# The first expert item's later rows: transposed by VectorE during the last query steps

## The chip, the core and the metric

The kernel runs on one core of a Trainium2 chip. Its time is the device time of one execution in microseconds; 267.24 us is the median of three runs, which lie between 267.22 and 270.07.

## The reference, cut to what matters

The inputs are q, k and v of shape 4 x 8 x 576 x 64 (batch, head, row, column), a random matrix omega of 128 x 64, and a mixture of eight experts with w1 of 512 x 1024 and w2 of 1024 x 512 each. All is float32.

```python
def phi(x):                                   # x = q or k, times 64 ** -0.25
    h = einsum('bhsd,md->bhsm', x, omega) - sum(x * x, -1) / 2
    return exp(h - max(h, -1)) / sqrt(128)
kv, z = einsum('bhsm,bhsd->bhmd', phi(k), v), sum(phi(k), 2)
attn = einsum('bhsm,bhmd->bhsd', phi(q), kv) / (einsum('bhsm,bhm->bhs', phi(q), z) + 1e-06)
x = attn.transpose(0, 2, 1, 3).reshape(2304, 512)
logits = x @ w_gate                           # 8 experts; each row goes to the largest
h = maximum(x_of_expert @ w1[e], 0)           # at most capacity = 576 rows for each expert
out[row] = gate[row] * (h @ w2[e])
```

## The kernel before, in words

**Attention.** The kernel first works through the keys in 18 steps, then through the 18 query tiles of 128 rows, in a software pipeline: step t projects tile t (`pjq`), transposes tile t - 2 on the matrix engine PE (`qtr`), turns it into phi(q) by exponentials on ScalarE (`qpT`, L798) and sums tile t - 3 against kv (`qacc`, L634). `normalise` (L645 to L660) then divides on VectorE, giving the tile `xr`, adds up the routing logits `lg` and stores the tile's rows in the DRAM tensor `x_d`. Steps 18 to 20 have no projection; the last two have fewer of the other parts. PSUM is scarce: `qtr` uses banks 3 and 4, `qacc` a single pair of banks, and the first layer of the experts goes round banks 0, 1 and 2.

**Experts.** Each batch of 576 rows is one item: the rows of a batch go to one expert. Four items run one after another. For an item the first layer (`mm1`, L668) has 16 groups: eight blocks `f` of 128 hidden columns times two halves of the rows, 256 and 320 of them. Every float32 product is made of three products of a high and a low part: `xhi` and `xlo` are the rows with features on partitions, `w1hi` and `w1lo` the weights. The high part comes from a copy on ScalarE with rounding, the low part from a subtraction on VectorE. After a group ScalarE writes the relu's high part (`hhii`, L680) and VectorE its low part (`hloi`, L683). The second layer (`mm2`, L842 to L844) gives `y`.

**The first item.** Its expert is read from the logits of row 0 as soon as tile 0 is done, so its weights load and are split (on GpSimd) during the query steps. Its rows 0 to 255 are taken from the tiles `xr` of query steps 3 and 4 while these are in SBUF: at steps 5 to 8 (`FIRST_AT`) PE transposes blocks of 64 rows beside the query transposes (`xtri`, L742), and `copy_x` makes the two parts. Rows 256 to 575 come back from `x_d`: at step 15 `first_rows` (L625) issues one load of 768 KB into `xg`, and ahead of the groups k = 0, 1 and 2 of the item's loop `transpose_x` has PE transpose 128, 128 and 64 of them (`xtri`, L398). Three groups, blocks 0 to 2 of the first half, are issued earlier, one in each of steps 18 to 20 (`AHEAD`); the loop begins with blocks 3 to 5 of the first half, and then comes block 0 of the second.

**Later items.** Their rows come by `load_x` (L380): four transfers, each for 32 partitions, which put rows in blocks of 32 with 512 bytes of a row in each partition (`xz`, a view of `xg`). `turn_x` (L386) transposes 32 x 32 blocks on VectorE into `xt`, ScalarE copies `xt` to `xhi` and VectorE subtracts to `xlo`. With it feature 4p + k lies on partition p in chunk k, so `load_w` loads these items' w1 by rows 4p + k, while the first item's features are 128k + p and its w1 is loaded in that order.

**Order.** The schedule is written by hand: each engine works off its instructions in the order of the program, and waits where an operand isn't ready. SyncE (SP) issues nearly all transfers, in the order of the program: at step 15 a store of `x_d`, then the rows; in the steps after it a store and a quarter of w2 each. Routing work of VectorE is spread over the first item's groups (`listing`).

Of the kernel before, what the change touches and what calls it, by code (L numbers as in the profile page):

```python
# [9 lines left out]
F32 = mybir.dt.float32  # L10
# [4 lines left out]
ALU = mybir.AluOpType  # L15
# [4 lines left out]
B, H, S, D, M = 4, 8, 576, 64, 128  # L20
# [4 lines left out]
SLOTS = 576  # L25
FIRST_CUTS = [0, 128, 384, 768, 1152]
SUB = 128
NSUB = 5
REST = SLOTS - 4 * SUB
NB, NBA = SLOTS // 32, 8  # L30
# [26 lines left out]
def attention_moe(ctx, tc, kT, qT, va, om, wg, w1, w2, cap, ident, tri, desc, lst, tab0, out):  # L57
    nc = tc.nc
# [8 lines left out]
    x_d = dram.tile([N + REST, DM], F32, name="x_d")  # L67
# [9 lines left out]
    SM = 5  # L77
# [272 lines left out]

    def load_w(i, c, ev, chunks_of="(k p)"):
        if i == 1:
            src = w1[ds(ev, 1), :, c * 256 : (c + 1) * 256].rearrange(f"o {chunks_of} f -> p (o k) f", p=128)
        else:
            src = w2[ds(ev, 1), c * 256 : (c + 1) * 256, :].rearrange("o (k p) f -> p (o k) f", p=128)
        nc.sync.dma_start(w_raw[i][c], src)
# [18 lines left out]
                in_offset=bass.IndirectOffsetOnAxis(ap=big["idx"][0:n, i, 2:3], axis=0),  # L377
            )

    def load_x(row):  # L380
        src = x_d[ds(row, SLOTS), :].rearrange("(b r) (q c) -> q r b c", r=32, q=4)
        for q in range(4):
            nc.sync.dma_start(big["xz"][32 * q : 32 * q + 32, :, :], src[q])


    def turn_x(b0, b1):  # L386
        t = big["xt"][:, 0 : b1 - b0, :].rearrange("p b (k r) -> p b k r", k=4)
        nc.vector.transpose(t, big["xz"][:, b0:b1, :].rearrange("p b (a k) -> p b k a", k=4))
        t = t.rearrange("p b k r -> p k b r")
        hi, lo = (big[x][:, :, 32 * b0 : 32 * b1].rearrange("p k (b r) -> p k b r", r=32) for x in ("xhi", "xlo"))  # L390
        nc.scalar.copy(hi, t)
        nc.vector.tensor_tensor(lo, t, hi.bitcast(F32), op=ALU.subtract)

    def transpose_x(i, nm, at):
        n = sub_n[i]
        tr = pair(f"xtr{nm}{i}") if at is None else bank(at, f"xtr{nm}{i}")
        for k in range(4):
            nc.tensor.transpose(  # L398
                tr[:, k * n : (k + 1) * n], big["xg"][0:n, i, k * 128 : (k + 1) * 128], id_sb[0:n, 0:n]
            )  # L400
        yield from copy_x(tr, i * SUB, n)
# [221 lines left out]
    xr_l = {}  # L623

    def first_rows():  # L625
        nc.sync.dma_start(
            big["xg"][:, 2:, :], x_d[2 * SUB : NSUB * SUB, :].rearrange("(i p) d -> p i d", p=SUB)
        )

    def numer(t, qpT, acc):  # L630
        for p in range(NP):
# [11 lines left out]

    def normalise(t, acc):
        xr = small.tile([128, ROW, H], F32, tag="xr", name=f"xr{t}", bufs=4)  # L645
        if t < 2:
            xr_l[t] = xr
        av = acc.rearrange("p (i x) -> p i x", i=2)[:, :, 0 : NP * ROW].rearrange("p i (h c) -> p c i h", c=ROW)
        den = small.tile([128, H], F32, tag="den", name=f"den{t}")
        nc.vector.tensor_scalar(den.rearrange("p (i h) -> p i h", i=2), av[:, D, :, :], EPS, None, op0=ALU.add)  # L650
        rec = small.tile([128, H], F32, tag="rec", name=f"rec{t}")
        nc.vector.reciprocal(rec, den)
        nc.vector.tensor_tensor(
            xr.rearrange("p c (i h) -> p c i h", i=2),
            av,
            rec.rearrange("p (i h) -> p i h", i=2).unsqueeze(1).to_broadcast([128, ROW, 2, NP]),
            op=ALU.mult,
        )
        nc.vector.tensor_reduce(lg[:, t, :], xr[:, D + 1 : ROW, :], op=ALU.add, axis=AX.X)
        nc.sync.dma_start(x_d[t * 128 : (t + 1) * 128, :], xr[:, 0:D, :].rearrange("p c h -> p (c h)"))  # L660

    HALVES = [(0, 256), (256, SLOTS)]

# [23 lines left out]
    def h_tiles(nm):  # L687
        return [
            hpool.tile([128, 8, w], dt, tag=t, name=f"{t}{nm}")
            for t, w, dt in (("hhi", 4 * SUB, F32R), ("hlo", 4 * SUB, F32R), ("hf", REST, F32))  # L690
        ]
# [8 lines left out]
    for n in range(NK + NT + 3):  # L700
# [20 lines left out]
        if 0 <= t - 2 < NT:  # L721
            d = d_l.pop(t - 2)
            trs = [bank(3 + i, f"qtr{n}{i}") for i in range(2)]

            parts = [
                [(trs[i][:, u * 64 : (u + 1) * 64], d[64 * i : 64 * i + 64, u, :], i) for u in range(H)] for i in range(2)
            ]

            if t in FIRST_AT:
                k0 = FIRST_AT.index(t)  # L730
                i = k0 % 2
                tr = bank(SM, f"xtri0{k0}")
                rows = slice(64 * i, 64 * i + 64)
                x0 = xr_l[k0 // 2][:, 0:D, :].rearrange("p c h -> p (c h)")
                parts[i][0:0] = [
                    (tr[:, k * 64 : (k + 1) * 64], x0[rows, k * 128 : (k + 1) * 128], i) for k in range(4)
                ]
                start(copy_x(tr, 64 * k0, 64))
            for x in chain(*zip_longest(*parts)):
                if x is not None:  # L740
                    rows = slice(64 * x[2], 64 * x[2] + 64)
                    nc.tensor.transpose(x[0], x[1], id_sb[rows, rows])  # L742
        if t == NT:
            h0 = h_tiles("i0")
        if t >= NT:
            mm1(*AHEAD[t - NT], *h0, "i0")
        run()

# [143 lines left out]
    with ExitStack() as ifs:  # L892
        for j in range(B):
            nm = f"i{j}"
            last = j == B - 1
            if j > 0:
                ifs.enter_context(tc.If(nd > j - 1))
            hhi, hlo, hf = h_tiles(nm) if j > 0 else h0
            if j > 0:
                row_a = nc.scalar.value_load(resd[0:1, 1, j - 1 : j], min_val=0, max_val=N - S)  # L900
            out_j = [out[0:SLOTS, :]] * 2 if j == 0 else [out[ds(r, SLOTS), :] for r in (row, row_a)]
            sc = sc_b[:, 0, :] if j == 0 else sc_j[:, j - 1, :]

            def put(i, n, y, out_j=out_j):

                k = int(i == NSUB - 2)
                (nc.sync, nc.scalar)[k].dma_start(out_j[k][i * SUB : i * SUB + n, :], y[0:n, :])

            def prefetch():
                nonlocal row  # L910
                if last:
                    return
                ev = nc.sync.value_load(resd[0:1, 0, j : j + 1], min_val=0, max_val=E - 1)
                row = nc.sync.value_load(resd[0:1, 1, j : j + 1], min_val=0, max_val=N - S)
                load_x(row)
                for c in range(4):
                    load_w(1, c, ev, "(p k)")
                yield
                for c in range(4):
                    load_w(2, c, ev)  # L920
                yield

            pre = prefetch()
            for k, (f, half) in enumerate(STEPS[j > 0]):

                if j == 0 and k < 3:
                    for _ in transpose_x(2 + k, nm, (SM, 3, None)[k]):
                        pass
                mm1(f, half, hhi, hlo, hf, nm)
                if j == 0:  # L930

                    listing(5 if k > 2 else 1)
                if j > 0 and k == 0:
                    next(pre, 0)
                if j == 0 and k < 6:
                    zero_out(k)
                if half == 0:
                    continue
                for i, c in HI_AT[j > 0].get(f, ()):
                    split_w_hi(i, c)  # L940
                for i, c in LO_AT[j > 0].get(f, ()):
                    split_w_lo(i, c)
            if j == 0:
                for _ in il:
                    pass
                next(pre, 0)
            for n, i in enumerate((NSUB - 1, *range(NSUB - 1))):
                pt = mm2(i, hhi, hlo, nm) if n > 0 else mm2_rest(hf, nm)
                if n == 0:
                    next(pre, 0)  # L950
                finish(i, pt, nm, sc[:, i : i + 1], put)

                if not last:
                    if n == 1:
                        turn_x(0, NBA)
                    for c in ((), (0,), (1,), (2, 3), ())[n]:
                        split_w_hi(1, c)
                        split_w_lo(1, c)
                    if n == 2:
                        turn_x(NBA, NB)  # L960
            if j == 0:
                nd = nc.values_load(resd[0:1, 2, 0:1], min_val=0, max_val=B - 1)
                nl = nc.values_load(resd[0:1, 2, 1:2], min_val=0, max_val=N)
# [68 lines left out]
    with ExitStack() as ifs:  # L1032
# [3 lines left out]
        for j in range(J):  # L1036
            nm = f"l{j}"
# [2 lines left out]
            sv = nc.sync.value_load(res[0:1, 1, j : j + 1], min_val=0, max_val=(E - 1) * REG + N)  # L1040
            load_idx(sv)
            for c in range(4):
                load_w(1, c, ev)
            for c in range(4):
                load_w(2, c, ev)
            gather()
# [71 lines left out]
```

## Time and profile before

| | |
|---|---|
| median of three runs | 267.24 us |
| profiled execution | 267.57 us |
| its span, first to last instruction | 265.7 us |
| PE busy | 257.0 us, 97% of the span |
| VectorE (DVE) busy | 166.2 us, 63% |
| ScalarE (ACT) busy | 150.5 us, 57% |
| GpSimd (POOL) busy | 36.6 us, 14% |

The profile is of one execution. Times in its rows are microseconds from the start of the span. PE is the matrix engine, SPq the transfer queue of SyncE. An arrow in a row goes from what is read to what is written, and L with a number is a line of the kernel. The chain of waits is followed back from the last instruction to what released each one, so a piece on it could not have begun sooner.

### The profile page before, as it was taken

How to read it: one execution, taken by the hardware profiler on the slowest of the kernel's cores; microseconds unless marked ns; L12 is line 12 of the kernel's file. 1: busy time of each engine (PE TensorE's matmuls, PEld its weight loads, DVE VectorE, ACT ScalarE, POOL GpSimd, SP SyncE). 2: the span in 40 equal slices, each digit the busy share in tenths (PEclk: the TensorE clock that was granted, in tenths of full speed). 3: DMA queues.
4: the chain of work that ended last, by engine and by line, in shares of the span. 5: the costliest groups of instructions: out<-in, count | busy, mean ns of one | idle time of the engine just before them, and what ended most of it. 6: DMA issues, size and time to landing. Idle time of an engine off the chain costs nothing.

```text
span 265.7 us, 7584 instructions
## 1 busy us (share of the span) xinstructions
PE 257.0 (97%) x3070; PEld 228.9 (86%) x3070; DVE 166.2 (63%) x329; ACT 150.5 (57%) x377; POOL 36.6 (14%) x54
## 2 busy tenths in 40 slices
PE   7999999999999999999999999999999999999990
PEld 6989999999999998999868889996888999958870
DVE  3889888869998984745762854443337443533570
ACT  4678878899999984436412465442254445224251
POOL 2100000243369892000000000000000000000000
PEclk9999999999999999999999999999999999999997
DMA  6999770045876677791079939900831892037211
GB/s 181 377 375 360 270 255 2 5 122 182 282 237 215 246 254 256 255 384 63 2 146 295 379 142 207 319 4 3 265 122 56 157 312 76 0 84 253 79 48 51
DMA packets 34130, 48.66 MB, mean 183 GB/s; under 512 B 2274, under 2 KB 21986, under 8 KB 34082
## 3 DMA queue, kind: packets, MB, share of 16 engines
q1 hardware_dynamic: 33506, 47.18, 56.2%
q10 hardware_dynamic: 576, 0.85, 0.9%
q8 instruction: 28, 0.46, 0.7%
q14 instruction: 20, 0.16, 0.2%
HBM read 36.10 MB, written 11.93 MB: 181 GB/s over the span
## 4 chain that ended last, share of the span: by engine, by line
PE 90%; ACT 3%; DVE 3%; issue 1%; ACTq 0%; DVEq 0%
PE hi L675 9%; PE hi L676 9%; PE hi L677 9%; PE yi L842 8%; PE pjk L165 8%; PE yi L843 8%; PE yi L844 8%; PE qacc L634 7%; PE pjq L165 6%; PE kacc L236 4%; PE kp L236 4%; PE qtr L742 3%; PE yi2r L854 1%; PE yi0r L854 1%; PE yi1r L854 1%
## 5 line engine op out<-in xcount | busy, mean ns | idle before, releaser
L675 PE MATMUL hi<-xhi,w1hi 128*128 128x256 f32 (+1 forms) x192 | 57.2, 298 | 0.3 <-DVE hloi L683 0.3
L676 PE MATMUL hi<-xhi,w1lo 128*128 128x256 f32 (+1 forms) x192 | 56.4, 294 | 0.0
L677 PE MATMUL hi<-xlo,w1hi 128*128 128x256 f32 (+1 forms) x192 | 56.3, 293 | 0.0
L683 DVE SCALAR_TENSOR_TENSOR hloi<-hi,hhii 128x256 fp32r<-128x256 f32 x48 | 20.2, 422 | 40.4 <-ACT hfi L682 24.5
L680 ACT ACTIVATE hhii<-hi 128x256 fp32r<-128x256 f32 x48 | 18.4, 385 | 42.8 <-PE hi L677 42.8
L842 PE MATMUL yi<-w2hi,hhii 128*128 128x512 f32 x96 | 37.7, 393 | 0.0
L843 PE MATMUL yi<-w2hi,hloi 128*128 128x512 f32 x96 | 37.4, 389 | 0.0
L844 PE MATMUL yi<-w2lo,hhii 128*128 128x512 f32 x96 | 37.4, 389 | 0.0
L675 PEld LDWEIGHTS hi<-xhi,w1hi 128*128 128x128 f32 x192 | 36.0, 188 | 0.8 <-DVE hloi L683 0.5
L676 PEld LDWEIGHTS hi<-xhi,w1lo 128*128 128x128 f32 x192 | 36.0, 188 | 0.1
L677 PEld LDWEIGHTS hi<-xlo,w1hi 128*128 128x128 f32 x192 | 36.0, 187 | 0.0
L182 DVE TENSOR_REDUCE mx<-pjk 128x4 f32<-128x512 f32 (+1 forms) x38 | 23.3, 654 | 5.5 <-PE pjk L165 5.5
L792 POOL TENSOR_TENSOR d<-d,mx 128x512 f32<-128x512 f32 x18 | 18.7, 1039 | 53.7 <-DVE mx L182 49.4
L165 PE MATMUL pjk<-om_s,kraw 64*128 64x128 f32 x288 | 24.9, 308 | 0.5 <-DVE ex L779 0.5
L773 ACT ACTIVATE ex<-pjk,mx 128x128 f32<-128x128 f32 x72 | 20.6, 368 | 7.4 <-DVE mx L182 7.2
L842 PEld LDWEIGHTS yi<-w2hi,hhii 128*128 128x128 f32 x96 | 18.0, 188 | 6.1 <-issue 2.4
L165 PEld LDWEIGHTS pjk<-om_s,kraw 64*128 64x128 f32 x288 | 21.3, 210 | 1.7 <-PE pjk L165 0.8
L634 PE MATMUL qacc<-kv_sb,qpT 128*64 128x73 f32 x576 | 22.5, 229 | 0.2 <-DVE e L587 0.2
L165 PE MATMUL pjq<-om_s,qraw 64*128 64x128 f32 x288 | 21.4, 284 | 0.1
L844 PEld LDWEIGHTS yi<-w2lo,hhii 128*128 128x128 f32 x96 | 18.0, 188 | 3.8
L634 PEld LDWEIGHTS qacc<-kv_sb,qpT 128*64 128x64 f32 x576 | 19.8, 136 | 1.6 <-PE qtr L742 0.3
L843 PEld LDWEIGHTS yi<-w2hi,hloi 128*128 128x128 f32 x96 | 18.0, 188 | 3.7
(141 smaller groups left out, 405.4 us busy)
## 6 DMA issues: line engine op xcount, KB each, us to landing
w1raw<-w SPq DMA_DIRECT2D x16, 512.0 KB, 8.3
w2raw<-w SPq DMA_DIRECT2D x16, 512.0 KB, 6.4
qraw<-qT SPq DMA_DIRECT2D x6, 768.0 KB, 6.3
x_d<-xr SPq DMA_DIRECT2D x18, 256.0 KB, 2.9
v<-va SPq DMA_DIRECT2D x7, 650.0 KB, 6.9
kraw<-kT SPq DMA_DIRECT2D x6, 576.0 KB, 6.6
xg<-x_d SPq DMA_DIRECT2D x12, 288.0 KB, 5.5
out<-zero_sb SPq DMA_DIRECT2D x4, 768.0 KB, 5.7
```

The costliest lines, as they stand in the source:

```text
L165: nc.tensor.matmul(banks[i][:, k * M : (k + 1) * M], parts[k][rows, :], om_s[rows, :], start=True, stop=True)
L182: nc.vector.tensor_reduce(mx[:, a : a + src.shape[1]], src, op=ALU.max, axis=AX.X, negate=True)
L236: nc.tensor.matmul(acc[f : f + 64, i * 2 * VW + o : i * 2 * VW + o + (z - a) * VW], ex[:, 4 * i + k, f : f + 64], v[:, i, a * VW : z * VW] ...
L634: nc.tensor.matmul(acc[r : r + 64, i * 512 + p * ROW : i * 512 + (p + 1) * ROW], qpT[:, r // 64, (4 * i + p) * 64 : (4 * i + p) * 64 + 64] ...
L675: nc.tensor.matmul(pt, whi_[:, k, fs], xhi[:, k, sl], start=(k == 0), stop=False)
L676: nc.tensor.matmul(pt, wlo_[:, k, fs], xhi[:, k, sl], start=False, stop=False)
L677: nc.tensor.matmul(pt, whi_[:, k, fs], xlo[:, k, sl], start=False, stop=(k == 3))
L683: nc.vector.scalar_tensor_tensor(hlo[:, f, sl], pt[:, 0:w], 0.0, hhi[:, f, sl].bitcast(F32), op0=ALU.max, op1=ALU.subtract)
L773: nc.scalar.activation(ex[:, o + k, :], q[0][:, k * M : (k + 1) * M], AF.Exp, bias=mx[:, o + k : o + k + 1], scale=1.0)
L842: nc.tensor.matmul(pt, hhi[:, f, sl], w2hi, start=(f == 0), stop=False)
L843: nc.tensor.matmul(pt, hlo[:, f, sl], w2hi, start=False, stop=False)
L844: nc.tensor.matmul(pt, hhi[:, f, sl], w2lo, start=False, stop=(f == 7))
```

## The change

The first item's rows 256 to 575 are loaded as the later items' rows are, by four transfers into blocks 8 to 17 of `xz`, at the same step 15. In steps 18, 19 and 20 `first_turn` transposes 4, 3 and 3 blocks on VectorE into `xt`, and ScalarE copies each part to `xhi`, ahead of that step's group of the first layer; the subtraction to `xlo` of a part follows one step later, ahead of the next part. PE's transposes L398 ahead of the groups k = 0 to 2 go. So that all features have the order 4p + k, the first two tiles' rows are copied by GpSimd from `xr` into `xt` with the features regrouped, and PE's transposes at steps 5 to 8 read that copy; the first item's w1 is loaded by rows 4p + k.

```diff
-    def load_w(i, c, ev, chunks_of="(k p)"):
+    def load_w(i, c, ev, chunks_of="(p k)"):
...
-    def load_x(row):
-        src = x_d[ds(row, SLOTS), :].rearrange("(b r) (q c) -> q r b c", r=32, q=4)
+    def load_x(rows, b0=0):
+        src = x_d[rows, :].rearrange("(b r) (q c) -> q r b c", r=32, q=4)
         for q in range(4):
-            nc.sync.dma_start(big["xz"][32 * q : 32 * q + 32, :, :], src[q])
+            nc.sync.dma_start(big["xz"][32 * q : 32 * q + 32, b0:, :], src[q])
-    def turn_x(b0, b1):
-        t = big["xt"][:, 0 : b1 - b0, :].rearrange("p b (k r) -> p b k r", k=4)
+    def turn_x(b0, b1, o=0):
+        t = big["xt"][:, o : o + b1 - b0, :].rearrange("p b (k r) -> p b k r", k=4)
         nc.vector.transpose(t, big["xz"][:, b0:b1, :].rearrange("p b (a k) -> p b k a", k=4))
         t = t.rearrange("p b k r -> p k b r")
         hi, lo = (big[x][:, :, 32 * b0 : 32 * b1].rearrange("p k (b r) -> p k b r", r=32) for x in ("xhi", "xlo"))
         nc.scalar.copy(hi, t)
-        nc.vector.tensor_tensor(lo, t, hi.bitcast(F32), op=ALU.subtract)
+        return lambda: nc.vector.tensor_tensor(lo, t, hi.bitcast(F32), op=ALU.subtract)
+    def first_turn():
+        lo = None
+        for b0, b1 in ((NBA, NBA + 4), (NBA + 4, NBA + 7), (NBA + 7, NB)):
+            if lo:
+                lo()
+            lo = turn_x(b0, b1, b0 - NBA)
+            yield
+        lo()
...
     def first_rows():
-        nc.sync.dma_start(
-            big["xg"][:, 2:, :], x_d[2 * SUB : NSUB * SUB, :].rearrange("(i p) d -> p i d", p=SUB)
-        )
+        load_x(slice(32 * NBA, SLOTS), NBA)
...
         nc.sync.dma_start(x_d[t * 128 : (t + 1) * 128, :], xr[:, 0:D, :].rearrange("p c h -> p (c h)"))
+        if t < 2:
+            xr_l[t] = big["xt"][:, 4 * t : 4 * t + 4, :]
+            nc.gpsimd.tensor_copy(xr_l[t], xr[:, 0:D, :].rearrange("p c h -> p (c h)").rearrange("p (m k) -> p k m", k=4))
...
-                x0 = xr_l[k0 // 2][:, 0:D, :].rearrange("p c h -> p (c h)")
+                x0 = xr_l[k0 // 2]
                 parts[i][0:0] = [
-                    (tr[:, k * 64 : (k + 1) * 64], x0[rows, k * 128 : (k + 1) * 128], i) for k in range(4)
+                    (tr[:, k * 64 : (k + 1) * 64], x0[rows, k, :], i) for k in range(4)
                 ]
...
         if t == NT:
             h0 = h_tiles("i0")
+            turner = first_turn()
         if t >= NT:
+            next(turner)
             mm1(*AHEAD[t - NT], *h0, "i0")
...
-                if j == 0 and k < 3:
-                    for _ in transpose_x(2 + k, nm, (SM, 3, None)[k]):
-                        pass
+                if j == 0 and k == 0:
+                    next(turner, 0)
                 mm1(f, half, hhi, hlo, hf, nm)
```

NBA is 8, NB is 18, NT is 18. The callers of `load_x`, `load_w` and `turn_x` in the later items are adapted so that they do what they did.

## Rows read from the trace of the kernel before

**Rows 1.** The page of the whole run: busy us, share of the span, instructions.

```profile
PE 257.0 (97%) x3070; PEld 228.9 (86%) x3070; DVE 166.2 (63%) x329; ACT 150.5 (57%) x377; POOL 36.6 (14%) x54
```

**Rows 2.** Chain of waits, 95 to 131 us: start us, us, engine, output, line.

```profile
100.63 0.99 ACT qpT L798 x2
101.66 0.71 PE qtr L742 x15
...
107.90 0.59 PE xtri L398 x4
...
109.90 0.44 PE xtri L398 x4
...
111.75 0.39 PE xtri L398 x4
```

**Rows 3.** PE in order of time, 93 to 125: start, us, instructions.

```profile
101.32 1.05 PE L742 MATMUL qtr<-id_sb,d 64*128 64x64 f32 x16
...
106.65 1.25 PE L634 MATMUL qacc<-kv_sb,qpT 128*64 128x73 f32 x32
...
113.59 0.31 PE L675 MATMUL hi<-xhi,w1hi 128*128 128x320 f32 x1
```

**Rows 4.** VectorE (DVE) in order of time; in brackets idle before, releaser.

```profile
99.07 0.22 DVE L659 TENSOR_REDUCE lg<-xr 128x8 f32<-128x64 f32 x1
100.66 0.42 DVE L683 SCALAR_TENSOR_TENSOR hloi<-hi,hhii 128x256 fp32r<-128x256 f32 x1 [1.37 <-ACT hhii L680]
...
102.67 0.22 DVE L659 TENSOR_REDUCE lg<-xr 128x8 f32<-128x64 f32 x1
104.43 0.42 DVE L683 SCALAR_TENSOR_TENSOR hloi<-hi,hhii 128x256 fp32r<-128x256 f32 x1 [1.54 <-ACT hhii L680]
...
107.17 0.42 DVE L683 SCALAR_TENSOR_TENSOR hloi<-hi,hhii 128x256 fp32r<-128x256 f32 x1 [0.51 <-ACT hhii L680]
```

**Rows 5.** ScalarE (ACT) in order of time, same stretch.

```profile
100.24 0.38 ACT L680 ACTIVATE hhii<-hi 128x256 fp32r<-128x256 f32 x1 [1.38 <-PE hi L677]
...
104.30 1.08 ACT L798 ACTIVATE qpT<-qtr 128x512 f32<-128x512 f32 x2
```

**Rows 6.** Groups by line and shape: busy us, mean ns of one, idle before.

```profile
L388 DVE STREAM_TRANSPOSE xt<-xg 128x1280 f32<-128x1280 f32 x3 | 7.3, 2440 | 0.0
L388 DVE STREAM_TRANSPOSE xt<-xg 128x1024 f32<-128x1024 f32 x3 | 6.0, 1991 | 5.8 <-DMA xg<-x_d 5.8
...
L410 DVE TENSOR_TENSOR xlo<-xtri,xhi 128x256 fp32r<-128x256 f32 x5 | 2.1, 416 | 0.0
L408 ACT CAST xhi<-xtri 128x256 fp32r<-128x256 f32 x5 | 1.9, 377 | 0.0
...
L410 DVE TENSOR_TENSOR xlo<-xtri,xhi 128x512 fp32r<-128x512 f32 x2 | 1.4, 687 | 0.0
...
L408 ACT CAST xhi<-xtri 128x512 fp32r<-128x512 f32 x2 | 1.2, 587 | 1.4 <-PE xtri L398 1.4
```

**Rows 7.** SyncE in order of time; DMA issues: count, KB each, us to landing.

```profile
93.92 0.43 SPq L626 DMA_DIRECT2D xg<-x_d  x1
...
133.76 2.01 SPq L383 DMA_DIRECT2D xg<-x_d  x4
...
xg<-x_d SPq DMA_DIRECT2D x1, 768.0 KB, 4.7
...
xg<-x_d SPq DMA_DIRECT2D x1, 288.0 KB, 3.8
...
xg<-x_d SPq DMA_DIRECT2D x1, 288.0 KB, 7.7
...
x_d<-xr SPq DMA_DIRECT2D x18, 256.0 KB, 2.9
```

**Rows 8.** GpSimd (POOL) in order of time, 54 to 73 and 93 to 125.

```profile
60.72 1.04 POOL L792 TENSOR_TENSOR d<-d,mx 128x512 f32<-128x512 f32 x1 [1.85 <-DVE e L593]
...
98.80 2.81 POOL L133 TENSOR_TENSOR w1lo<-w1raw,w1hi 128x256 fp32r<-128x256 f32 x4
```

More of the change, by code (lines that the diff above doesn't have):

```diff
@@ L645, in normalise @@
         xr = small.tile([128, ROW, H], F32, tag="xr", name=f"xr{t}", bufs=4)
-        if t < 2:
-            xr_l[t] = xr
         av = acc.rearrange("p (i x) -> p i x", i=2)[:, :, 0 : NP * ROW].rearrange("p i (h c) -> p c i h", c=ROW)
@@ L914, in prefetch @@
                 row = nc.sync.value_load(resd[0:1, 1, j : j + 1], min_val=0, max_val=N - S)
-                load_x(row)
+                load_x(ds(row, SLOTS))
                 for c in range(4):
-                    load_w(1, c, ev, "(p k)")
+                    load_w(1, c, ev)
                 yield
@@ L954, in attention_moe @@
                     if n == 1:
-                        turn_x(0, NBA)
+                        turn_x(0, NBA)()
                     for c in ((), (0,), (1,), (2, 3), ())[n]:
@@ L959, in attention_moe @@
                     if n == 2:
-                        turn_x(NBA, NB)
+                        turn_x(NBA, NB)()
             if j == 0:
@@ L1042, in attention_moe @@
             for c in range(4):
-                load_w(1, c, ev)
+                load_w(1, c, ev, "(k p)")
             for c in range(4):
```

## The prediction

> **What bounds the kernel now.** I read the busy times first [rows 1]: the matrix engine works 257.0 of 265.7 us, so a change counts by what it takes from, or puts into, PE's order of work; work of another engine counts where PE waits for it. Then the chain of waits from the last query steps to the first item [rows 2]. The reader is to see two things. The three groups of PE transposes (xtri) lie on the chain, 0.59 + 0.44 + 0.39 = 1.42 us. And ahead of them the chain leaves PE: ScalarE's relu (hhii, 100.24 [rows 5]) and then its two exponentials (qpT, 0.99) end last, and PE's next query transposes take up again at 101.66. In PE's order of time [rows 3] these transposes start at 101.32, behind the sums of query tile 15, and last 1.05 us. They write the PSUM banks that the exponentials read. ScalarE has no slack there.
>
> **What goes.** The twelve xtri transposes: 1.42 us of the chain [rows 2]. The four rank-1 groups that follow have nothing else to wait for, so all of it is a gain on PE. ScalarE's and VectorE's halves of the same splits don't go, they move ahead.
>
> **What comes, first of three parts.** The first query step without a projection now begins, on VectorE, with a 32x32 transpose of 128x512, and on ScalarE with a copy of it to xhi, and this copy stands ahead of the relu and of the exponentials. VectorE's last work of the step before ends at 99.07 + 0.22 = 99.29 [rows 4]; it then idles 1.37 us, and ScalarE idles 1.38 us ahead of its relu at 100.24 [rows 5]. No 128x512 transpose is in the trace. The two forms that are [rows 6], 1024 columns in 1.99 us and 1280 in 2.44, give 1.75 ns for a further column, so 1.09 us for 512 and 0.87 for 384 (estimates). The copy of 512 takes 0.59 by the cast that it replaces [rows 6]. With L for the time at which VectorE can start (it is free and the rows have landed), the relu starts at L + 1.09 + 0.03 + 0.59 = L + 1.71, where it started at 100.24. What is queued behind the copy on ScalarE is that relu and both exponentials, and PE's transposes wait for these: PE loses L - 98.53 us, one for one. Minus 1.42, the kernel moves by **L - 99.95 us**.
>
> [...] The two rows say 1.75 ns a column, and the sum goes by them.
>
> **When do the rows land?** Before, one transfer of 768 KB, issued at 93.92, landed after 4.7 us [rows 7], at 98.6, and nobody waited. Now four transfers take its place, one for each 32 partitions, of 160 KB each. The same pattern with 288 KB each is in the trace: four issues in 2.01 us from 133.76, so 0.50 apart. The first lands 3.8 us after its issue and the last 7.7 after its own, 9.2 after the first. That is (9.2 - 3.8)/3 = 1.8 us for 288 KB, so 1.0 for 160 KB; the first quarter would land after 3.8 - 0.8 = 3.0 and the last after 6.0, at 99.9. A store of x_d issued just ahead is in the same queue. I take L = 100.0 (an estimate). Bounds: below, VectorE's own 99.29; above, the whole 9.2 us of the larger load, 103.1, if what counts is the traffic around it.
>
> **Second and third part.** VectorE gets the subtraction of part one (0.69, by the same operation on 512 columns) and a transpose of 384 (0.87), 1.56 us, before the relu's remainder (hloi) of the second step, where it idled 1.54 [rows 4]; ScalarE gets a copy of 384, 0.48 between 0.59 and 0.38. Counted from the end of lg at 102.89, and as if PE hadn't moved, the copy ends at 102.89 + 1.56 + 0.03 + 0.48 = 104.96; the relu and the exponentials of query tile 17 behind it, which ended at 105.38 [rows 5], come at most 0.9 us late and end by 106.3, ahead of the sums that read them, 106.65 [rows 3]. Those sums also need their PSUM pair, which VectorE frees by normalising tile 16 behind the late hloi; by the same count that comes between 0.1 us early and 0.3 late. I take 0 and keep 0.3 for the range. In the third step VectorE gets 0.55 + 0.87 = 1.42 against an idle 0.51 [rows 4], so it is 0.9 us late; behind it stand the normalisation of tile 17 (2.23 us from hloi to the end of lg, as for tile 15) and the last subtraction, 0.55, which end at 107.17 + 0.91 + 2.23 + 0.55 = 110.9. The first to need them is the second half's first group, at 113.59 before [rows 3] and 1.42 earlier now, 112.2. PE and VectorE are late together, so the cover of 1.3 us holds. Cost: nothing.
>
> **The rest.** *The copies of the first two tiles' rows on GpSimd*, 128x512 with a step of four: a two-input pass over as many elements takes 1.04 us; I take 1 us and hold 0.5 to 2 possible. GpSimd idles 1.85 us ahead of its pass at 60.72 [rows 8], from the moment that the rows are ready; above 1.85 the pass is late, and its users come two steps on. Nothing. *w1 by rows 4p + k*: pieces of 1 KB as before, from other addresses, in loads that end steps before use. Nothing. *SyncE* issues three transfers more, some 1.5 us, behind which stand a store and a load of w2, first used in the second layer. Nothing. In the first item's opening steps ScalarE and VectorE lose their part of the splits, where PE didn't wait for them.
>
> **Sum.** -1.42 + (100.0 - 98.53) = +0.05 us on the profiled execution's 267.57 (span 265.7). The median of the three runs is 267.24, 0.33 below it; I give the time against the median: 267.24 + 0.05, rounded to 267.3.
>
> **The rivals.**
> 1. *The rows land while VectorE is still busy.* A transfer of 768 KB landed in 4.7 us, and the new one has fewer bytes: L = 99.29, net -0.66, 266.6 us. Against it: the rate of four transfers to 32 partitions each. No case can give more, as VectorE is not free sooner.
> 2. *They land late*: the side on which the kernel is slower. Place: the transpose at the head of VectorE's queue, and behind it ScalarE's copy, relu and exponentials. Every microsecond of L above 99.95 is one of PE's. For it: the pattern took 9.2 us for 1152 KB, and stores and w2 follow it in the queue. L = 102.0 gives 269.3, L = 103.1 gives 270.4; it is slower by over 1% only from L = 102.6.
> 3. *The load doesn't start when the program says.* If reading x_d by column groups has to wait for the store issued just ahead, it starts a store's landing, 2.9 us [rows 7], later: L near 102.5, net +2.5, 269.8. Against it: the one transfer of before was issued at once, and the slots are the same.
> 4. *GpSimd stands in VectorE's way.* GpSimd subtracts w1 from 98.80 to 101.61 in four passes [rows 8]; a transpose that must let one finish starts up to 0.7 us late: +0.75, 268.0. [...] No row here shows a transpose beside GpSimd.
>
> **How the numbers follow.** Forecast (L from 99.6 to 101) 0.55, rival 1 0.22, rival 2 0.14, rival 3 0.04, rival 4 0.05. The range leaves out the late end of rivals 2 and 3 and a little below rival 1: low 266.0 is rival 1 less the 0.36 us of a quicker transpose and a little for the spread of runs (0.35 between the profiled execution and the fastest), high 268.9 is L = 101.6. One per cent, 2.7 us, is about what a measurement of this kernel can tell from no change: under 264.6 none of these cases comes, 0.02 for what I don't see; over 269.9 only L above 102.6, half of rival 3 and a fifth of rival 2, 0.05; between, 0.93.
>
> **What would show it.** After: no xtri from xg on PE; in its place an idle time of PE ahead of the query transposes of tile 17, that ends with the exponentials, 1.2 to 1.9 us later than before. ScalarE's copy of 512 starts as VectorE's transpose ends, and that starts with a DMA as its releaser at 99.6 to 101. A transpose of 512 at 1.0 to 1.2 us, of 384 at 0.8 to 0.95. The first group of the second half at 113.6 give or take 0.8. I am wrong if PE doesn't wait there (the copy was hidden), if the wait is over 2.5 us, or if the difference arises anywhere after the first item's first half.

## The result, and the profile after

The changed kernel takes **269.05 us** (median of 22 runs, 267.68 to 272.56) against 267.23 for the kernel before (22 runs beside them): ratio 1.0064, interval 1.0045 to 1.0083. It is 0.6% slower. Here and below, medians take in all runs, and ratios leave out those over 1.5% above the fastest of their kernel (3 of these 22, 3 of the 12 of e6, 1 of the 12 of e9). The forecast was 267.3 with 268.9 as its upper end, so the time lies just outside. The execution profiled after took 270.71 us, 1.66 above its median, with a span of 268.9, against 267.57 and 265.7.

To see where the 3.14 us between the two profiled executions lie, I cut both at rows that each of them has: the query transposes of tile 16 (their row of 0.89 us), the first 320-column group (the second half of the first item), the start of the last write of `ysi`, and the last instruction.

| stage | before | after | difference |
|---|---|---|---|
| span's start to the transposes of tile 16 | 97.71 | 97.34 | -0.37 |
| to the first group of the second half | 15.88 | 18.39 | **+2.51** |
| the four items, to the start of their last write of `ysi` | 145.73 | 145.40 | -0.33 |
| from there to the end | 6.4 | 7.77 | **+1.37** |

The start and the middle vary like this without any change to them: in the profiles of this document the transposes of tile 16 begin between 97.34 and 98.63 us, and e8 below, which runs the same instructions as the kernel before, has 145.28 us for the four items against 145.73. What the change did is in the two bold rows.

First the busy times, which answer to [rows 1]: twelve matmuls fewer, three VectorE and two GpSimd instructions more, 1.7 us less of PE.

```profile
PE 255.3 (95%) x3058; PEld 227.5 (85%) x3058; DVE 168.4 (63%) x332; ACT 150.4 (56%) x377; POOL 38.9 (14%) x56
```

The chain of waits of the kernel after, which answers to [rows 2] (start us, us, what):

```profile
95.08 5.44 DMA xg<-x_d
...
100.64 1.11 DVE xt L388
...
101.77 0.62 ACT xhi L391
102.39 0.28 ACT hhii L690
102.67 0.98 ACT qpT L810 x2
...
103.70 0.80 PE qtr L752 x15
```

The `xtri` pieces are gone. In their place the chain leaves PE earlier and runs through the last quarter of the rows, the transpose, the copy, the relu and the exponentials: the path that the prediction drew, with a transfer at its head. PE in order of time, as in [rows 3] (start, us, instructions; in brackets idle before and what ended it):

```profile
103.26 0.24 PE L752 MATMUL qtr<-id_sb,d 64*128 64x64 f32 x1 [2.25 <-issue]
103.70 0.80 PE L752 MATMUL qtr<-id_sb,d 64*128 64x64 f32 x15 [0.20 <-ACT qpT L810]
104.44 0.58 PE L685 MATMUL hi<-xhi,w1hi 128*128 128x256 f32 x1
...
107.29 1.36 PE L642 MATMUL qacc<-kv_sb,qpT 128*64 128x73 f32 x32
...
115.73 0.31 PE L685 MATMUL hi<-xhi,w1hi 128*128 128x320 f32 x1
```

PE idles 2.25 + 0.20 us ahead of the query transposes of tile 17. After that the group of twelve matmuls at 104.44 lasts until 107.29, 2.85 us; the same group lasts 1.61 in the run with PE kept busy, below. Why, the granted clock says (per stretch: its length, busy time and instructions of five engines, then the granted clock, DMA share, GB/s):

```profile
103.00:104.00 1.00, 0.54 (x9) 0.43 (x11) 0.93 (x4) 0.65 (x2) 0.00 (x0) 1.00 0.06 23
104.00:105.00 1.00, 1.00 (x15) 0.88 (x12) 0.97 (x3) 0.00 (x0) 0.00 (x0) 0.59 0.00 0
105.00:106.00 1.00, 1.00 (x7) 1.00 (x6) 0.89 (x2) 0.08 (x1) 0.00 (x0) 0.50 0.86 283
...
107.00:108.00 1.00, 1.00 (x20) 0.78 (x21) 0.18 (x1) 0.60 (x2) 0.00 (x0) 0.71 0.72 281
```

After the idle time TensorE's clock is granted at half (0.59, 0.50, 0.50 and 0.71 of full speed in the four stretches from 104 to 108) for some three microseconds of dense work, and from 108 to 109 at 1.00 again. A product of 256 columns takes 0.41 us from 104.81 to 106.95, and 0.28 from 108.81.

VectorE and ScalarE in the same stretch, as in [rows 4] and [rows 5]:

```profile
100.64 1.10 DVE L388 STREAM_TRANSPOSE xt<-xg 128x512 f32<-128x512 f32 x1 [1.73 <-DMA xg<-x_d]
...
105.01 0.87 DVE L388 STREAM_TRANSPOSE xt<-xg 128x384 f32<-128x384 f32 x1
```

```profile
101.77 0.62 ACT L391 CAST xhi<-xt 128x512 fp32r<-128x512 f32 x1 [3.28 <-DVE xt L388]
102.30 0.38 ACT L690 ACTIVATE hhii<-hi 128x256 fp32r<-128x256 f32 x1
102.57 1.07 ACT L810 ACTIVATE qpT<-qtr 128x512 f32<-128x512 f32 x2
```

VectorE is free from 98.92 and starts when the rows have landed. The sizes are as estimated: 1.10 us for 512 columns and 0.87 for 384. SyncE's issue of the rows and the landing of its four transfers, which answer to [rows 7], and GpSimd's copies, to [rows 8]:

```profile
93.55 1.99 SPq L383 DMA_DIRECT2D xg<-x_d  x4
```

```profile
xg<-x_d SPq DMA_DIRECT2D x4, 160.0 KB, 3.2
...
xg<-x_d SPq DMA_DIRECT2D x1, 160.0 KB, 2.7
...
xg<-x_d SPq DMA_DIRECT2D x1, 160.0 KB, 5.4
```

```profile
58.64 1.15 POOL L670 COPY xt<-xr 128x512 f32<-128x512 f32 x1
60.49 1.04 POOL L804 TENSOR_TENSOR d<-d,mx 128x512 f32<-128x512 f32 x1 [0.70 <-DVE e L603]
```

The four quarters together have a median of 3.2 us from issue to landing; the two rows below it are the first and the last quarter alone. The first three take 2.7, 3.1 and 3.4 us, and only the last one takes the 5.44 of the chain. GpSimd still idles 0.70 us behind the copy: that part is hidden.

The end of the run is the other bold row. These are barrier instructions of PE's weight queue, and after the change one of SyncE too, at the program's last line (count, min/median/max ns, start of the first and of the last), first before, then after:

```profile
L1114 PEldq DRAIN  x2: 8/8/8, 264.2 to 265.2; - x2
...
L1114 PEldq EVENT_SEMAPHORE  x2: 51/51/51, 265.1 to 265.7; - x2
```

```profile
L1124 SPq DRAIN  x3: 7/7/13, 266.4 to 266.7; - x3
...
L1124 PEldq DRAIN  x2: 8/8/8, 265.4 to 268.7; - x2
...
L1124 PEldq EVENT_SEMAPHORE  x2: 51/51/51, 266.6 to 268.9; - x2
```

Before, PE goes from its semaphore at 265.1 to its drain at 265.2. After, from 266.6 to 268.7: PE is 2.0 us late between two successive barrier instructions, with nothing to compute, and the run ends only behind it. The waits of SyncE say the same, 0.5 us for PE at the longest before and 2.2 after (in total, times, longest):

```profile
SPq L1114 <- PEq L1114: 0.7, 2, 0.5
...
SPq L1124 <- PEq L1124: 2.4, 2, 2.2
```

### The profile page after: what moved, and what is told of

It reads as the page before. It is cut to its first block, busy times and chain, and to the rows that moved or that the text cites. A ratio compares the mean times of both kernels' runs of the same rounds, so it can differ in the third digit from the quotient of the medians.

```text
span 268.9 us, 7568 instructions
## 1 busy us (share of the span) xinstructions
PE 255.3 (95%) x3058; PEld 227.5 (85%) x3058; DVE 168.4 (63%) x332; ACT 150.4 (56%) x377; POOL 38.9 (14%) x56
## 4 chain that ended last, share of the span: by engine, by line
PE 83%; DMA 5%; ACT 3%; SPq 3%; DVE 2%; issue 1%; DVEq 0%
PE hi L685 10%; PE hi L686 9%; PE hi L687 9%; PE yi L854 8%; PE yi L855 8%; PE yi L856 8%; PE qacc L642 6%; PE pjq L165 5%; PE pjk L165 5%; PE kp L236 3%; PE kacc L236 3%; DMA kraw<-kT 3%; PE qtr L752 3%; DMA xg<-x_d 2%; PE yi2r L866 1%; PE yi1r L866 1%
## 5 line engine op out<-in xcount | busy, mean ns | idle before, releaser
L687 PE MATMUL hi<-xlo,w1hi 128*128 128x256 f32 (+1 forms) x192 | 56.9, 296 | 0.0
L685 PEld LDWEIGHTS hi<-xhi,w1hi 128*128 128x128 f32 x192 | 36.6, 190 | 0.6
L686 PEld LDWEIGHTS hi<-xhi,w1lo 128*128 128x128 f32 x192 | 36.6, 191 | 0.1
L687 PEld LDWEIGHTS hi<-xlo,w1hi 128*128 128x128 f32 x192 | 36.6, 190 | 0.0
L165 PE MATMUL pjk<-om_s,kraw 64*128 64x128 f32 x288 | 23.2, 291 | 1.9 <-DMA kraw<-kT 1.2
L165 PEld LDWEIGHTS pjk<-om_s,kraw 64*128 64x128 f32 x288 | 19.7, 195 | 3.1 <-DMA kraw<-kT 1.4
L391 ACT CAST xhi<-xt 128x1024 fp32r<-128x1024 f32 (+3 forms) x9 | 8.6, 953 | 22.9 <-DVE xt L388 22.9
```

The source lines that it names most:

```text
L165: nc.tensor.matmul(banks[i][:, k * M : (k + 1) * M], parts[k][rows, :], om_s[rows, :], start=True, stop=True)
L685: nc.tensor.matmul(pt, whi_[:, k, fs], xhi[:, k, sl], start=(k == 0), stop=False)
L686: nc.tensor.matmul(pt, wlo_[:, k, fs], xhi[:, k, sl], start=False, stop=False)
L687: nc.tensor.matmul(pt, whi_[:, k, fs], xlo[:, k, sl], start=False, stop=(k == 3))
```

## The experiments

Each was run twelve times beside the kernel before on the same chip, except e2, which was run once. e4 and e8 are edits of the kernel before, the others of the changed kernel. Four questions: does PE lose what the rows are late by; is the slower group the granted clock's; what makes the end late; and what is left when all three are taken away.

**The rows one step later, and two steps earlier.**

```diff
-FIRST_LOAD = 15
+FIRST_LOAD = 16      # e2_load16
+FIRST_LOAD = 13      # e1_load13
```

> The changed kernel with the rows loaded one query step later, at step 16. If VectorE's start is set by the landing, one for one: its first transpose starts some 2.8 us later than in the changed kernel and PE's idle time ahead of the query transposes of tile 17 grows from 2.25 to about 5; the granted clock falls after it; the time rises by 2.8 to 4. If something else holds VectorE: no change.

One execution, 277.82 us. PE and the granted clock:

```profile
108.12 1.55 PE L752 MATMUL qtr<-id_sb,d 64*128 64x64 f32 x16 [6.26 <-issue]
```

```profile
103.00:104.00 1.00, 0.00 (x0) 0.00 (x0) 0.00 (x0) 0.00 (x0) 0.00 (x0) 1.00 1.20 248
104.00:105.00 1.00, 0.00 (x0) 0.00 (x0) 0.00 (x0) 0.00 (x0) 0.00 (x0) 0.51 1.05 265
...
113.00:114.00 1.00, 1.00 (x22) 1.00 (x20) 0.41 (x1) 0.93 (x2) 0.00 (x0) 0.50 0.06 16
```

VectorE waits 5.75 us for the rows instead of 1.73, and PE's idle time ahead of the transposes is 6.26 instead of 2.25: 4.02 and 4.01, one for one. Both are longer than expected (2.8 and about 2.75), and so is the time: the stage up to the second half takes 5.03 us more than in the changed kernel. The clock falls to half while PE still idles and stays there for some ten microseconds, about six of them with PE at work.

> The changed kernel with the later rows loaded two query steps earlier (step 13 for 15), so that they have landed long before VectorE is free. Theory A (the rows land late and PE pays every microsecond of it; a fall of the granted clock after PE's idle time comes on top): the transpose of 512 starts when VectorE is free, with no DMA as its releaser; PE idles 0.8 to 1.2 us ahead of the query transposes of tile 17 instead of 2.25; the granted clock stays at 1.00 there; 266.6 us, 0.7 below the kernel before. Theory B (the place of ScalarE's copy ahead of relu and exponentials is the loss, whenever the rows land): PE's idle stays above 2 us and the time at about 269. Theory C (the loss is the load's traffic or the new order of the features): no change, about 269.

268.61 us, ratio 1.0044 (1.002 to 1.0067). The transpose starts at 99.41, at VectorE's own time, without a wait for a DMA; PE idles 0.49 + 0.20, the group behind takes 1.62 us (1.61 in e3, below, at a granted clock of 1.00), and the stage up to the second half takes 15.14 us, 0.74 less than before. Yet the kernel is 2 us above the expected time and slower than before: its end takes 8.05 us. The rows' lateness is not the only cause.

**PE kept busy through its wait (e3).** Six float32 products into a spare bank stand behind the sums of tile 15, ahead of the query transposes of tile 17; their result is not used.

```diff
+            if t == NT:
+                fb = bank(SM, "fill")
+                for _ in range(6):
+                    nc.tensor.matmul(fb[:, 0:192], warm[:, 0:128], warm[:, 0:192], start=True, stop=True)
```

> The changed kernel with six matmuls of zeros (128x192, float32, their result unused) put into PE's order between the sums of tile 15 and the query transposes of tile 17, where PE idled 2.25 us. If the clock is a cost of its own: the granted clock stays at 1.00, the next group of the first layer takes 1.6 us again instead of 2.85, the wait for the exponentials stays, and the time is 0.7 to 1.5 below the changed kernel, 267.6 to 268.3. Rival (the clock only accompanies the wait, or its fall has another cause): group still 2.85 us, time 269 or, with the added work, above.

268.41 us, ratio 1.0049 (1.0022 to 1.0075). PE in order of time:

```profile
101.32 2.22 PE L778 MATMUL fill<-warm 128*128 128x192 f32 x12
104.04 0.24 PE L752 MATMUL qtr<-id_sb,d 64*128 64x64 f32 x1 [0.50 <-issue]
104.48 0.71 PE L752 MATMUL qtr<-id_sb,d 64*128 64x64 f32 x15 [0.20 <-ACT qpT L814]
105.13 0.39 PE L685 MATMUL hi<-xhi,w1hi 128*128 128x256 f32 x1
...
106.74 1.25 PE L642 MATMUL qacc<-kv_sb,qpT 128*64 128x73 f32 x32
```

The exponentials still decide when PE goes on, but the granted clock is 1.00 throughout, and the group behind takes 1.61 us (105.13 to 106.74). So the slower group is the clock's, and with PE at work through the wait the clock did not fall in this execution. With the rows later than in the run of the kernel after (VectorE waits 2.13), the stage is 1.42 us longer than before instead of 2.51. The time is 0.1 above the expected range, and it doesn't measure the clock alone: the fill counts as twelve instructions on PE, which runs 3070 as before, and SyncE's last wait for PE is 0.5 us again. So this kernel is rid of the late end too.

**The order of features alone (e4).** Loads, placement and PE's transposes as before; only w1 by rows 4p + k, GpSimd's copies, and PE's transposes of `xg` read every fourth column.

```diff
-    def load_w(i, c, ev, chunks_of="(k p)"):
+    def load_w(i, c, ev, chunks_of="(p k)"):
...
+        xk = big["xg"][0:n, i, :].rearrange("p (m k) -> p k m", k=4)
...
-                tr[:, k * n : (k + 1) * n], big["xg"][0:n, i, k * 128 : (k + 1) * 128], id_sb[0:n, 0:n]
+                tr[:, k * n : (k + 1) * n], xk[:, k, :], id_sb[0:n, 0:n]
...
```

> The kernel before with the features' order alone changed: w1 of the first item by rows 4p + k, GpSimd's regrouping copies of the first two tiles, and PE's transposes of the later rows kept, on every fourth column. Theory A: these parts are hidden; 267.2, within 0.4 of the kernel before. Theory C (GpSimd's copies or w1's other addresses cost something): at least 1 us above the kernel before, 268.2 or more, with PE waiting at steps 5 to 8 or at the first groups of the first layer.

267.62 us, ratio 1.0004 (0.9983 to 1.0024). The chain's pieces of the three groups that [rows 2] has at 0.59, 0.44 and 0.39:

```profile
108.00 0.68 PE xtri L399 x4
...
110.10 0.49 PE xtri L399 x4
...
112.00 0.62 PE xtri L399 x4
```

0.37 us more for the strided read, which the changed kernel doesn't have; the stage is 0.33 longer. The order of w1 and GpSimd's copies cost nothing that shows within the interval, as predicted.

**ScalarE's copy behind the exponentials (e5).** The rows are loaded at step 13, and the copy of a part stands behind the step's relu and exponentials instead of ahead of them.

```diff
-            lo = turn_x(b0, b1, b0 - NBA)
+            hi, lo = turn_x(b0, b1, b0 - NBA, True)
+            yield
+            hi()
             yield
...
+            if t >= NT:          # behind the exponentials
+                next(turner)
```

> The changed kernel with the rows loaded at step 13, and ScalarE's copy of each part moved behind that step's relu and exponentials. Theory A with the place of the copy as the second term: PE waits no longer than the kernel before did there (0.35), so the whole 1.42 us of the removed transposes is gained, 265.8. If the place of the copy costs nothing: as the run with the early load alone. If late work of VectorE (subtraction and transpose of 384 ahead of the normalisation) is what comes next: PE waits for the PSUM pair in steps 19 and 20, and less than 1 us is gained.

268.14 us, ratio 1.0013 (0.9993 to 1.0033). The stage takes 14.47 us, 1.41 less than before: the transposes' 1.42 with no wait in their place. But again the end takes 8.2 us, and the time is 2.3 above the expected 265.8 and not under that of before.

**PE's program, longer and shorter.** The kernel has a branch for inputs that need lists of rows; these inputs skip it. The changed kernel has twelve transposes fewer on PE, so its program is shorter. First (e6) the changed kernel with twelve transposes put into the skipped branch:

```diff
+        pb = bank(SM, "pad")
+        for k in range(12):
+            m = SUB if k < 8 else REST
+            nc.tensor.transpose(pb[0:m, 0:m], id_sb[0:m, 0:m], id_sb[0:m, 0:m])
```

> The changed kernel with twelve PE transposes (8 of 128x128, 4 of 64x64) put into the branch for left-over rows, which is not taken here: no work is added, only PE's program gets its old length back. Theory D (PE's program, now 12 transposes shorter, ends at a place where its last instructions come late: SyncE's wait for PE at the program's end went from 0.5 to 2.2 us in the changed kernel, and stayed 0.5 in the run with six more matmuls): that wait is 0.5 again and the time falls by 1.6, to 267.5. Rival (the end's 1.6 us is chance of single executions, or hangs on what PE did before): wait still about 2, time 269.

268.74 us (266.08 to 271.94), ratio 1.001 (0.998 to 1.004) against 267.55. SyncE's last wait for PE is 0.5 us again:

```profile
SPq L1128 <- PEq L1128: 0.7, 2, 0.5
```

In this execution PE idled 1.93 + 0.20 us and the clock did not fall; the stage was 0.69 us longer than before. The late end is gone, but the median is 1.2 us above the expected 267.5, and the runs are as spread as those of the changed kernel: the time alone would not settle the question.

Then (e8) the kernel before, with twelve transposes fewer in the skipped branch, and the three copies of ScalarE and three subtractions of VectorE that go with them; nothing else is touched:

```diff
-            for i in range(NSUB):
+            for i in range(NSUB if j < J - 1 else 2):
```

> The kernel before with twelve PE transposes (and the three copies and subtractions that go with them) left out of the last of the lists in the branch for left-over rows, which is not taken here: nothing that runs is changed, PE's program is as much shorter as the change makes it. Theory D: SyncE's wait for PE at the program's end goes from 0.5 to about 2, the time rises by 1.6, to 268.9. Rival: 267.3, as the kernel before.

268.70 us against 267.55, ratio 1.0042 (1.0025 to 1.0059). The barrier rows:

```profile
L1114 PEldq DRAIN  x2: 8/8/8, 263.6 to 264.6; - x2
...
L1114 SPq EVENT_SEMAPHORE  x14: 17/28/28, 263.5 to 265.0; - x14
...
L1114 PEldq EVENT_SEMAPHORE  x2: 51/51/51, 264.4 to 266.9; - x2
```

All that runs is as before up to the end (the stage takes 15.88 us in both), and SyncE is through at 265.0; PE's last semaphore comes at 266.9. In the changed kernel PE is late between semaphore and drain, here between drain and semaphore; what fixes the place is not shown. Over all profiles the rule has no exception: of the five kernels with twelve PE instructions fewer the changed one, e1, e5 and e8 have PE 1.7 to 2.0 us behind SyncE at the end, and in e2 SyncE's longest wait for PE is 2.2, as in the changed one; of the seven with the old number six (before, e3, e6, e7, e9, e10) have SyncE's longest wait for PE there at 0.5, and the seventh, e4, ends 6.2 us after the start of its last write of `ysi`, against 6.4 before. As e6 adds to PE alone, it is PE's program that counts, and not ScalarE's or VectorE's.

**All three taken away, and two of them.** e7 is e5 with the twelve transposes in the skipped branch; e9 is e7 with the rows loaded at step 15, as in the changed kernel; e10 is e6 with the rows loaded at step 13.

> Rows loaded at step 13, ScalarE's copies behind relu and exponentials, and PE's program padded in the branch that isn't taken. If the terms add up (1.42 us of transposes gained, no new wait, no late end): 265.8, 1.4 below the kernel before. If the end isn't a matter of the program's length: 267.5 to 268.

**266.61 us** against 267.55, ratio 0.9964 (0.9944 to 0.9985). It is faster than the kernel before, by 0.94 us where 1.4 was expected. PE doesn't wait; ScalarE has its copy behind the exponentials:

```profile
100.55 1.25 PE L647 MATMUL qacc<-kv_sb,qpT 128*64 128x73 f32 x32
101.72 1.05 PE L757 MATMUL qtr<-id_sb,d 64*128 64x64 f32 x16
```

```profile
100.65 0.38 ACT L695 ACTIVATE hhii<-hi 128x256 fp32r<-128x256 f32 x1 [1.38 <-PE hi L692]
100.93 1.08 ACT L815 ACTIVATE qpT<-qtr 128x512 f32<-128x512 f32 x2
101.89 0.63 ACT L393 CAST xhi<-xt 128x512 fp32r<-128x512 f32 x1
```

> The changed kernel with ScalarE's copies behind the relu and the exponentials and PE's program padded in the branch that isn't taken, but the rows loaded at step 15 as in the change. If the wait needs both (late rows and the copy ahead of the exponentials): VectorE's transpose still starts after a DMA, some 1 to 1.7 us after VectorE is free, but PE no longer waits for it at the query transposes of tile 17; the normalisation of tile 15 behind the transpose delays the next sums by 0 to 0.5 us; 266.0 to 266.5. If late rows alone make PE wait: PE idles about 2 us again, 267.5 to 268.5.

266.75 us against 267.24, ratio 0.9972 (0.9955 to 0.9988), 0.25 above the expected range. The rows land late here too, and PE hardly waits for them:

```profile
101.74 1.12 DVE L388 STREAM_TRANSPOSE xt<-xg 128x512 f32<-128x512 f32 x1 [2.22 <-DMA xg<-x_d]
```

```profile
101.55 1.05 PE L757 MATMUL qtr<-id_sb,d 64*128 64x64 f32 x16
...
104.42 1.25 PE L647 MATMUL qacc<-kv_sb,qpT 128*64 128x73 f32 x32 [0.20 <-DVE xr L664]
```

The query transposes don't wait. What is queued behind the late transpose on VectorE, the relu's low part and the normalisation, costs PE 0.20 us there and 0.21 in the next step. The stage takes 15.07 us, 0.60 more than in e7.

> The changed kernel with the rows loaded at step 13 and PE's program padded, ScalarE's copies ahead of the relu as in the change. By the sum of the prediction with VectorE's start at its own time: PE idles about 0.7 us ahead of the query transposes of tile 17, no fall of the clock, 0.66 below the kernel before, 266.6 to 266.9. Rival (the place of the copy is the whole loss): 268 or more.

267.03 us against 267.24, ratio 1.0001 (0.9979 to 1.0023). The stage is 0.75 us shorter than before, the end 0.13 longer; of that the timed runs show 0.2 at most. The sign is as expected, but no gain is established.

## Why the prediction was wrong

**The chain of the first part was right.** The prediction said that the kernel moves by L - 99.95 us, with L the time at which VectorE can start. With L taken from each run's own start of the first transpose, shifted so that the transposes of tile 16 stand at 97.71 as before:

| kernel | L | L - 99.95 | stage, against 15.88 | granted clock |
|---|---|---|---|---|
| e1, rows at step 13 | 99.25 | -0.70 | -0.74 | group behind 1.62 us, at 1.00 in e3 1.61 |
| e10, rows at step 13 | 99.24 | -0.71 | -0.75 | group behind 1.61 us |
| e6, changed, longer program | 100.68 | +0.73 | +0.69 | 1.00 |
| e3, PE kept busy | 101.42 | +1.47 | +1.42 | 1.00 |
| after | 101.01 | +1.06 | +2.51 | fell to 0.50 |
| e2, rows at step 16 | 105.04 | +5.09 | +7.54 | fell to 0.50 |

Where the clock stays, by its own figure or by the length of the group behind the wait, the formula holds to 0.05 us over a range of 2.2, in four single executions. All the estimates in it stand: the transpose of 512 took 1.10 (1.09), the copy 0.62 (0.59), the gain from the twelve `xtri` transposes 1.41 (1.42). The low end of the range also holds 0.36 us for a quicker transpose. No run shows that term: the transpose of 512, which reads every fourth element, took 1.10 us (after), 1.12 (e1) and 1.08 (e2); going by the rows was right.

**The step that failed first is the landing: "I take L = 100.0".** It was 101.0 in the profiled execution, and 100.7 and 101.4 in two others with the same load. The prediction let each further quarter of 160 KB cost 1.0 us, 160/288 of the 1.8 measured in the larger load. For the first three quarters that was right or too long: they landed 2.7, 3.6 and 4.4 us after the first issue, where the count gives 3.0, 4.0 and 5.0. But from the first issue at 93.55 the last quarter landed at 95.08 + 5.44 = 100.52, after 6.97 us instead of 6.0, 2.5 behind the third. In e3, e6 and e9, with the load at the same step, the chain has a quarter that lands late too: 5.8, 5.1 and 5.9 us after its issue, where in e9 the four have a median of 3.4. What holds it is not shown; a store and a quarter of w2 are issued behind it, at 95.93 and 96.48. Only the size of this term was off, and its upper bound of 103.1 held; rival 2, the late side, is what happened, in a mild form: +1.06 us. With L = 101.0 in place of 100.0 the sum gives 268.3, still inside the range. So the late landing alone doesn't carry the time past 268.9.

**The granted clock was not in the sum at all.** The prediction had PE go on 1.2 to 1.9 us later than before and priced that idle time at its own length. The transposes behind the exponentials came 2.41 us later (103.70 against 101.66 [rows 2], and the 0.37 by which this execution was ahead), which is L - 98.53 to within 0.07; and the work behind them then ran at half clock (0.50 granted from 105 to 107). In the profiled execution this is 2.51 - 1.06 = 1.45 us, more than the late rows themselves. After 2.25 us of idle (after) and within 6.26 (e2) the clock fell; after 1.93 (e6) and 0.50 (e3, filled) it stayed at 1.00. That is one execution each, so the idle time as the cause of the fall is argued and not shown, and how much idle PE may have is open. The timed runs don't settle it. Of the changed kernel's 22 runs the six with a mean granted clock under 0.989 all take 270.7 us or more, and e7, without the wait, lies close together (265.12 to 267.37); but e3, which kept its clock in its profiled execution, is spread from 267.77 to 271.34.

**The end was not in it either.** The prediction called itself wrong if the difference arises anywhere after the first item's first half: 1.37 us of it did. With the landing it takes the time out of the range; neither does so alone. The prediction counted the transposes that go as time, and not as instructions of PE's program; what their absence does at the end it put, without a word, at nothing. e8 shows that it costs 1.15 us of the median even in code that never runs; e6, e7 and e10 show that putting twelve back gives it back: ratios 1.0064 to 1.001 (after, e6), 1.0044 to 1.0001 (e1, e10), 1.0013 to 0.9964 (e5, e7), each taken beside the kernel before. What holds PE up is not shown. The pages list transfers of instructions (queue q8: 28 of them with 0.46 MB, so 16 KB each, in the kernel before and after alike). In the kernel after one of these is under way from 265.7 to about 267.1, over the start of PE's late stretch (266.6 to 268.7), and in e8 from 264.4 to about 265.4; but one runs near the end of the kernels before, e1, e6 and e7 as well, in the kernel before from 264.6 to about 265.5 with PE on time, and the traces don't say which engine it is for.

**The other rivals.** Rival 1 (rows land while VectorE is busy, -0.66) is what e1 and e10 have in that stage, -0.74 and -0.75. Rival 3 (the load held by the store) did not show: SyncE issued at 93.55, and the first quarter landed 2.7 us later, where that rival waits 2.9 before it starts. Rival 4 (GpSimd in VectorE's way, 0.75) is out: in e1 the transpose starts as soon as VectorE is free, at 99.41, and takes 1.12 us, all beside GpSimd's subtraction of w1 (98.96 to 101.77); it takes 1.08 in e2 with GpSimd idle. The second and third part, SyncE's issues and GpSimd's copies cost nothing, as said; the copies took 1.15 us against the 1 assumed. Of the signs that the prediction named, the DMA as releaser and the sizes came true; the first group of the second half, forecast for 113.6 give or take 0.8, came at 115.73.

**The sum of the profiled execution**, with what was measured: 1.06 (late rows, net of the transposes) + 1.45 (clock) + 1.37 (end) - 0.37 - 0.33 (start and middle, chance) = 3.18 us of span; the span grew by 3.2. The median moved by only 1.82. Of this e8 accounts for 1.15, and the late rows cost 0.73 to 1.47 in the three executions of the table with the load at step 15 (e6, after, e3): these two already fill it, so the clock's 1.45 belongs to the profiled execution, and no run shows that the median has a part of it.

## What to carry to other kernels

Work that moves to another engine should stand behind, not ahead of, what the bounding engine waits for, above all when its input comes by a transfer that might be late: the same late rows cost PE 0.4 us of waits with the copy behind the exponentials and 2.45 with it ahead. Price an idle gap that you put into a dense matrix stretch by its length, and look at the granted clock for half-clock work behind it: in the profiled execution here that was 1.45 us more. After a change of the number of instructions look at the last microseconds of every engine (here 1.37 us of the difference) before you explain the rest, and put a few unused instructions in or out to see whether the end moves.

## What the runs showed of the hardware that was not expected

- Twelve matrix instructions fewer in a branch that isn't taken (with six fewer of other engines) made the kernel 1.15 us slower (e8, median 268.70 against 267.55); of the five kernels that are shorter by twelve, in four (after, e1, e5, e8) PE's late barrier instruction comes 1.7 to 2.0 us behind SyncE's, and in the fifth (e2) SyncE waits 2.2 us for PE.
- After 2.25 us of idle PE the granted clock was at 0.50 to 0.71 for some 3 us of dense matmuls; after 1.93 us it was at 1.00. In a gap of 6.26 us it fell before PE went on, and stayed at half for about six more. Each is one execution.
- Four transfers of 160 KB to 32 partitions each took 6.97 us from the first issue to the last landing, where the one transfer of 768 KB of before took 4.7; the last of the four alone took 5.44.
- The float32 transposes on PE that read every fourth column took longer (e4, one execution): the three groups had 0.68, 0.49 and 0.62 us on the chain instead of 0.59, 0.44 and 0.39.
